# Pipelining three layer boundaries by groups of four slots, with the last channels of the first convolution in two small blocks

## Chip, cores, metric

One core of one Trainium2 chip. The metric is the device time of one execution of the program, in microseconds; the times below are medians of several executions. Before the change it was 617.7 us (three runs, 616.61 to 618.29). A "span" is the time from the first to the last instruction in a profiled execution; it is about 1.8 us shorter than the device time of the same execution.

## The reference, cut

```python
x = u                                              # 2048 positions x 512 channels, bf16
x = x + conv(layernorm(x), A, B, C, log_dt, Dskip)  # long convolution per channel: kernel K from A, B, C
x = x + attn(layernorm(x), wqkv, wo)                # 32 heads of 16, 8 keys at distance 0, 2, .. 14
x = x + conv(layernorm(x), ...)                     # the same convolution again
x = x + attn(layernorm(x), wqkv, wo)                # the same attention again
# conv: y = irfft(rfft(pad(x)) * rfft(pad(K)))[:L] + x * Dskip
```

The kernel runs as four stages: tables and the convolution's spectra together with the first convolution (until about 265 us), attention (until about 402), second convolution (until about 470), attention (until the end). Three boundaries lie between them, and each needs a layer norm over all 512 channels of a position. The state `X` is held as 16 "slots" of 128 positions, `X[:, j, :]`.

## The kernel before: the parts the change touches

The layer norm statistics. `gather` takes statistics of a stretch of channels, `finish` aggregates them and makes scale and bias, `norm` applies them:

```python
    def gather(self, X, part, j0, j1): ...      # nc.vector.bn_stats, one per slot
    def finish(self, j0, j1):
        for j in range(j0, j1):
            nc.vector.bn_aggr(self.mv[:, j, :], ...)
        nc.vector.tensor_copy(self.mvb[:, js], self.mv[:, js])
        nc.vector.tensor_scalar(self.veps[:, js], self.mvb[:, js, 1], EPS, None, ALU.add)
        nc.scalar.activation(self.den[:, js], self.veps[:, js], ACT.Sqrt)
        nc.vector.reciprocal(self.rstd[:, js], self.den[:, js])
        nc.vector.scalar_tensor_tensor(self.nb[:, js], self.mvb[:, js, 0], -1.0, self.rstd[:, js], ...)
```

The end of the first convolution. Channels 448 to 511 are the last "half": tables, contraction into the convolution kernel, spill to memory and refetch in another layout, spectrum `Kt`, products with the signal's spectrum, inverse, final matmuls, then the norm over all 16 slots:

```python
        cv.finish(3, xc, Kt, Xr, 0, 2)          # channels 384..447
        ln_b.gather(X, 0, 0, NJ)                # three quarters of the channels, 16 slots
        Kt = k_fft(3, 1, 2)                     # spectrum of the last 64 channels, at once
        cv.finish(3, xc, Kt, Xr, 2, 4)
        ln_b.gather(X, 1, 0, NJ)
        ln_b.finish(0, NJ)
```

The weights of the attention. The value weights are loaded and re-laid by four VectorE copies, which the scheduler places behind the last statistics:

```python
        nc.scalar.dma_start(wvn[:], wsrc[:, :, 1024:1536])
        for ft in range(4):
            nc.vector.tensor_copy(wv[:, :, ft*128:(ft+1)*128]..., wvn[:, :, ft*128:(ft+1)*128]...)
```

The second convolution, with the norm in front of it and the statistics behind it:

```python
        for j in range(0, NJ, 4): ln.gather(X, 0, j, j + 4)
        ln.finish(0, NJ)
        for j in range(NJ): ln.norm(U[:, j, :], X[:, j, :], j)
        for k in range(16 + 14):
            ...                                  # final, inverse, product, s2, turn, s1, staggered
            if k == 13 + 11: ln_b.gather(X, 0, 0, NJ)
        ln_b.gather(X, 1, 0, NJ)
        ln_b.finish(0, NJ)
```

In the second convolution `U` is the normalised signal, `ps_s` and `Z` the first stage of its transform, `pt` and `zt` its transpose, `xp` and `xc` the second stage, `pa`, `pb` and `Y` the product with the kernel's spectrum `Kt`, `vp` and `VT` the inverse, and `ps_y` the last stage. `psA` is memory of the same kind that several of these steps share. In the attention, 16 normalised slots are transposed (tile `pt_x`), projected to queries and keys (`ps_qk`, evacuated by ScalarE into `qT` and `kT`), multiplied (`prod`), and summed into logits (`Lp`); then come the value projection (`ps_v`), softmax, `po` and the output projection (`ps_o`, evacuated into `X`).

## Time and profile before

| | before |
|---|---|
| time, median of 3 | 617.7 us |
| profiled span | 613.9 us |
| tables end (last `Y2tab` product) | 230.7 |
| first attention: first transpose `pt_x` | 271.7 |
| first output evacuation | 378.6 |
| second convolution: first / last `xp` | 414.2 / 460.7 |
| second attention: first transpose `pt_x` | 478.7 |

The times in the lower rows are microseconds from the start of the span. The page of the kernel before opens with busy time, share of the span and instruction counts by engine:

```profile
span 613.9 us, 13332 instructions
PE 447.4 (73%) x5785; PEld 288.1 (47%) x5785; DVE 508.0 (83%) x921; ACT 337.5 (55%) x452; POOL 12.7 (2%) x49
```

The shares are averages over stages with different limits. The timeline of VectorE (DVE) around the first boundary follows. The columns are start, busy time, engine, line, operation, output<-inputs, shapes, count, and in brackets the idle time in front of it with what ended it.

```profile
230.63 7.45 DVE L140 BATCH_NORM_STATS2 ln_st_b<-X 128x6 f32<-128x384 bf16 x16
...
253.99 2.19 DVE L114 COPY wv<-wvn 128x512 bf16<-128x512 bf16 x4 [13.10 <-DMA wvn<-in_B_wqkv_dram]
256.10 0.68 DVE L254 TENSOR_TENSOR pa<-xc,Kt 128x1024 bf16<-128x1024 bf16 x1
...
265.66 3.19 DVE L140 BATCH_NORM_STATS2 ln_st_b<-X 128x6 f32<-128x128 bf16 x16 [7.08 <-ACT X L270]
268.77 1.28 DVE L145 BATCH_NORM_AGGREGATE ln_mv_b<-ln_st_b 128x2 f32<-128x12 f32 x16
...
271.25 1.70 DVE L153 TENSOR_SCALAR xn<-X,ln_rstd_b,ln_nb_b 128x512 bf16<-128x512 bf16 x5
```

For 13.10 us VectorE stands before the weight copies, whose load has not landed. The last spectrum was complete at 253.73, but the first product `pa` needs only the first of its two casts, which ended at 252.82. So `pa`, which started at 256.10, was held up for 3.3 us: about 1.2 by the load and 2.1 by the copies themselves. After that everything is serial: products, inverse, final matmuls, 16 statistics, 16 aggregates, the small steps, the first norm. TensorE (PE) in the same place:

```profile
256.84 0.40 PE L239 MATMUL psA<-sb_IC,pa 128*128 128x256 bf16 x1 [4.20 <-DVE pa L254]
...
258.06 0.42 PE L239 MATMUL psA<-sb_IC,pa 128*128 128x256 bf16 x1
258.27 0.42 PE L240 MATMUL psA<-sb_IC,pb 128*128 128x256 bf16 x1
```

The matmuls of this kind start 0.21 us apart after the idle time; before it, at full clock, the same matmuls came 0.11 apart. The granted clock was 0.50 from about 255 to 261.8. TensorE's idle time in front of these matmuls was 4.20 us (252.64 to 256.84), and the clock was halved about 2.3 us into it (see the last section).

The boundary to the second convolution, VectorE and then TensorE: 16 norms in a row, and TensorE waits 3.31 us for the first.

```profile
404.70 5.26 DVE L153 TENSOR_SCALAR U<-X,ln_rstd_a,ln_nb_a 128x512 bf16<-128x512 bf16 x16
```

```profile
405.17 1.34 PE L591 MATMUL ps_s_6063<-U,sb_F_128 128*128 128x128 bf16 x8 [3.31 <-DVE U L153]
```

The boundary from the second convolution to the attention, VectorE and then TensorE: 27 statistics and 16 aggregates stand ahead of the first norm, and TensorE idles 8.60 us.

```profile
467.60 8.24 DVE L140 BATCH_NORM_STATS2 ln_st_b<-X 128x6 f32<-128x384 bf16 x27
475.75 1.28 DVE L145 BATCH_NORM_AGGREGATE ln_mv_b<-ln_st_b 128x2 f32<-128x12 f32 x16
...
478.24 1.71 DVE L153 TENSOR_SCALAR xn<-X,ln_rstd_b,ln_nb_b 128x512 bf16<-128x512 bf16 x5
```

```profile
478.71 4.00 PE L693 MATMUL pt_x<-sb_ident,xn 128*128 128x128 bf16 x32 [8.60 <-DVE xn L153]
```

### The profile page before, as it was taken

The numbers are of one execution on the slowest core, as the hardware profiler recorded it, in microseconds if no ns is written. First come the engines' busy times: TensorE is split into PE (matmuls) and PEld (weight loads), VectorE is DVE, ScalarE is ACT, GpSimd is POOL, SyncE is SP. The second block draws the span as 40 slices with busy tenths as digits, with TensorE's granted clock in tenths as the row PEclk, the third lists the DMA queues.
The fourth block names the chain that finished last, engine by engine and source line by source line (L and its number), as shares of the span: only waits on it lengthen the run. The fifth ranks groups of instructions, "written<-read, shape, count | busy, mean of one in ns | idle before, by whom it ended". The sixth has DMA issues, their size and how long they took to land.

```text
span 613.9 us, 13332 instructions
## 1 busy us (share of the span) xinstructions
PE 447.4 (73%) x5785; PEld 288.1 (47%) x5785; DVE 508.0 (83%) x921; ACT 337.5 (55%) x452; POOL 12.7 (2%) x49
## 2 busy tenths in 40 slices
PE   1101867767777777559988679969995799957996
PEld 0101544554564465344333566646773533326763
DVE  5999799999999996265977899768999678879950
ACT  4999357556554654437575223467874456732144
POOL 0000000000000000300000000000000000000000
PEclk9999999898897898879999699979999799977999
DMA  9101001311221042500002100060000000040011
GB/s 292 61 1 34 19 19 37 103 38 36 88 53 36 21 121 72 171 1 1 1 1 82 39 1 1 1 275 1 1 2 1 2 1 0 1 120 1 1 70 68
DMA packets 23048, 28.77 MB, mean 47 GB/s; under 512 B 13009, under 2 KB 18514, under 8 KB 21838
## 3 DMA queue, kind: packets, MB, share of 16 engines
q1 hardware_dynamic: 20590, 26.75, 13.1%
q10 hardware_dynamic: 2400, 1.18, 0.7%
q8 instruction: 45, 0.74, 0.5%
q14 instruction: 13, 0.11, 0.1%
HBM read 15.89 MB, written 8.39 MB: 40 GB/s over the span
## 4 chain that ended last, share of the span: by engine, by line
DVE 49%; PE 34%; issue 8%; ACT 5%; DMA 3%; POOL 0%; SPq 0%; POOLq 0%; DVEq 0%; ACTq 0%
PE ps_qk L711 9%; DVE Ytab L443 5%; PE ps_v L721 5%; DVE ta L412 4%; PE ps_o L835 4%; DVE tb L413 4%; DVE Y2tab L445 4%; PE po L826 2%; DVE Xtab L414 2%; DVE ln_st_b L140 2%; PE Lp L753 2%; DVE Ytab L414 2%; DVE pa L620 2%; DVE pb L621 1%; DVE VT L643 1%
## 5 line engine op out<-in xcount | busy, mean ns | idle before, releaser
L711 PE MATMUL ps_qk<-xnT,wqk 128*128 128x512 bf16 x256 | 63.1, 382 | 0.9 <-ACT kT_4648 L713 0.3
L829 ACT CAST oT<-po 128x1024 bf16<-128x1024 f32 x16 | 15.4, 1015 | 58.7 <-PE po L826 58.7
L187 PE MATMUL psA<-X,sb_F_128 128*128 128x128 bf16 x128 | 15.1, 236 | 36.5 <-ACT X L498 32.6
L187 PEld LDWEIGHTS <-sb_F_128 128*128 128x128 bf16 x288 | 17.6, 99 | 46.8 <-issue 44.1
L835 PE MATMUL ps_o<-wo_t,oT 128*128 128x512 bf16 x128 | 34.6, 380 | 3.4 <-ACT oT L829 2.6
L711 PEld LDWEIGHTS <-wqk 128*128 128x128 bf16 x256 | 22.9, 98 | 29.5 <-issue 8.2
L174 ACT CAST Z<-psA 128x1024 bf16<-128x1024 f32 (+1 forms) x36 | 31.1, 930 | 8.9 <-PE psA L187 8.7
L462 PE MATMUL psk<-Y2tab,Xtab 128*32 128x48 bf16 x1024 | 22.8, 201 | 16.5 <-issue 15.2
L459 PE MATMUL psk<-Ytab,Xtab 128*32 128x64 bf16 x1024 | 24.1, 205 | 12.5 <-DVE Xtab L414 5.5
L753 PE MATMUL Lp<-prod,sb_bones 128*32 128x512 bf16 x256 | 24.7, 392 | 10.3 <-DVE prod L748 7.5
L174 ACT CAST VT<-psA 128x512 bf16<-128x512 f32 x32 | 17.2, 589 | 23.6 <-PE psA L242 23.6
L443 DVE TENSOR_TENSOR Ytab<-Ytab,MA 128x2048 bf16<-128x2048 bf16 x24 | 29.3, 1220 | 0.2
L462 PEld LDWEIGHTS <-Xtab 128*32 128x32 bf16 x1024 | 20.2, 100 | 19.5 <-issue 18.1
L445 DVE TENSOR_TENSOR Y2tab<-Ytab,MB 128x2048 bf16<-128x2048 bf16 x24 | 29.2, 1218 | 0.0
L721 PE MATMUL ps_v<-wv,xnT 128*128 128x512 bf16 x128 | 28.3, 379 | 0.0
L459 PEld LDWEIGHTS <-Xtab 128*32 128x32 bf16 x1024 | 20.7, 103 | 15.0 <-issue 13.6
L140 DVE BATCH_NORM_STATS2 ln_st_b<-X 128x6 f32<-128x384 bf16 (+1 forms) x64 | 21.4, 413 | 7.1 <-ACT X L270 7.1
L838 ACT CAST X<-ps_o 128x512 bf16<-128x512 f32 x32 | 18.3, 586 | 16.0 <-PE ps_o L837 16.0
L202 PE MATMUL pt<-sb_ident,Z 128*128 128x128 bf16 x256 | 21.7, 239 | 7.2 <-ACT Z L174 7.2
L140 DVE BATCH_NORM_STATS2 ln_st_a<-X 128x6 f32<-128x512 bf16 x32 | 21.1, 687 | 7.1 <-ACT X L838 5.3
L465 ACT CAST KTq<-psk 128x1024 bf16<-128x1024 f32 x8 | 8.1, 1013 | 32.1 <-issue 16.6
L693 PE MATMUL pt_x<-sb_ident,xn 128*128 128x128 bf16 x128 | 13.5, 266 | 15.0 <-DVE xn L153 14.8
(462 smaller groups left out, 1311.1 us busy)
## 6 DMA issues: line engine op xcount, KB each, us to landing
Kt<-kt_scratch SPq DMA_DIRECT2D x4, 1024.0 KB, 6.7
Vp<-V SPq DMA_DIRECT2D x2, 1568.0 KB, 9.2
kt_scratch<-Kt SPq DMA_DIRECT2D x3, 1024.0 KB, 4.5
X<-in_A_u_dram SPq DMA_DIRECT2D x4, 512.0 KB, 5.5
Xr<-in_A_u_dram SPq DMA_DIRECT2D x4, 512.0 KB, 4.5
k_scratch<-KTq SPq DMA_DIRECT2D x8, 256.0 KB, 2.1
KT<-k_scratch SPq DMA_DIRECT2D x8, 256.0 KB, 3.6
out_dram<-X SPq DMA_DIRECT2D x4, 512.0 KB, 2.6
```

Source lines behind the costliest of these rows:

```text
L140: self.nc.vector.bn_stats(self.st[:, j, part, :], X[:, j, a:b])
L174: self.nc.scalar.copy(dst, src)
L187: nc.tensor.matmul(o, F1[:, j, r, :], rhs_j(j), start=True, stop=not dk)
L412: nc.vector.tensor_tensor(v(ta), src, self.mult(self.MA, lev, hc, mm), ALU.mult)
L443: nc.vector.tensor_tensor(Y[:, :, :, q * EYB:(q + 1) * EYB, :].rearrange("n c h e t -> n (c h) e t"), src, self.mult(self.MA, lev, hc, EYB ...
L445: nc.vector.tensor_tensor(Y2[:, :, :, (q - 1) * EYB:q * EYB, :].rearrange("n c h e t -> n (c h) e t"), src, self.mult(self.MB, lev, hc, EY ...
L459: nc.tensor.matmul(psk[32 * g:32 * g + 32, ds, :], xs, Y[:, m // 2, h, :, t], start=(m == 0), stop=False, skip_group_check=True)
L462: nc.tensor.matmul(psk[32 * g:32 * g + 32, ds, EYB:], xs, Y2[:, 1 - m // 2, h, :, t], start=False, stop=(m == 3), skip_group_check=True)
L711: nc.tensor.matmul(ps[:], wqk[:, ct, f0:f0 + 128], xnT[:, ct, s0:s0 + 512], start=(ct == 0), stop=(ct == 3))
L721: nc.tensor.matmul(ps[:].rearrange("p a b -> p (a b)"), xnT[:, ct, j * 128:(j + 1) * 128], wv[:, ct, :], start=(ct == 0), stop=(ct == 3))
L753: nc.tensor.matmul(Lp[r0:r0 + 32, w // 4, :], bones[:, w % 4, :], pr[:, f2, hb * 512:(hb + 1) * 512], start=(w % 4 == 0), stop=(w % 4 == 3 ...
L835: nc.tensor.matmul(ps[:], oT[:, ft, j * 128:(j + 1) * 128], wo_t[:, ft, :], start=(ft == 0), stop=False)
```

## The change

The intent is to turn each boundary from "all 16 slots, then the next layer" into four groups of four slots: statistics, aggregate, scale and norm of a group follow as soon as its four slots are final, and the next layer starts on it. In addition the last 64 channels of the first convolution are cut into two blocks of 32 which are contracted, spilled, fetched and transformed separately, with half as many inverse matmuls per block (VectorE combines the two products first). The value weights' copies move to ScalarE, into the place in the program where the value projection starts. A block `with at(tc, mark)` gives instructions an earlier priority for the scheduler, which is how a group's norms are placed in the layer before. The core of the diff:

```diff
@@ load_b_weights
-        nc.scalar.dma_start(wvn[:], wsrc[:, :, 1024:1536])
-        for ft in range(4):
-            nc.vector.tensor_copy(wv[...], wvn[...])
+    nc.sync.dma_start(wvn[:], wsrc[:, :, 1024:1536])
@@ proj_v (in the attention)
+            for ft in range(4 if wvn is not None else 0):
+                nc.scalar.copy(wv[...], wvn[...])
@@ LnStats.finish
-        nc.vector.tensor_copy(self.mvb[:, js], self.mv[:, js])
-        nc.vector.tensor_scalar(self.veps[:, js], self.mvb[:, js, 1], EPS, None, ALU.add)
-        nc.scalar.activation(self.den[:, js], self.veps[:, js], ACT.Sqrt)
+        nc.scalar.activation(self.den[:, js], self.mv[:, js, 1], ACT.Sqrt, bias=self.eps[:, 0:1])
@@ end of the first convolution
-        Kt = k_fft(3, 1, 2)
-        cv.finish(3, xc, Kt, Xr, 2, 4)
-        ln_b.gather(X, 1, 0, NJ)
-        ln_b.finish(0, NJ)
+        T.y_products(Y, Y2, 7, 0, HD // 2)
+        T.y_products(Y, Y2, 7, HD // 2, HD)
+        ...
+            T.contract(Xt, Y, Y2, 7, 0)
+            T.contract(Xt, Y, Y2, 7, 1)
+        ...
+            for u in range(2):
+                nc.sync.dma_start(KT[:, u]..., kscr[7][:, :, u * 128:u * 128 + 128]...)
+                cv.spectrum32(KT[:, u], ..., Kt[:, 2 + u], ...)
+                cv.block(2 + u, xc, Kt, VT)
+        def after(j0, j1):
+            ln_b.gather(X, 2, j0, j1)
+            ln_b.finish(j0, j1)
+            marks.append(room(tc, 40))
+        cv.final(3, 64, 128, Xr, VT, 4, after)
@@ second convolution: norms by groups in front, statistics by groups behind
+        for q in range(4):
+            with at(tc, marks[q]):
+                for j in range(q * 4, q * 4 + 4):
+                    ln.norm(U[:, j, :], X[:, j, :], j)
...
-            if k == 13 + 11:
-                ln_b.gather(X, 0, 0, NJ)
-        ln_b.gather(X, 1, 0, NJ)
-        ln_b.finish(0, NJ)
+            q = k - 13 - 8
+            if 0 <= q < 4:
+                ln_b.gather(X, 0, q * 4, q * 4 + 4)
+            elif 4 <= q:
+                ln_b.gather(X, 1, (q - 4) * 4, q * 4 - 12)
+                ln_b.finish((q - 4) * 4, q * 4 - 12)
+                marks.append(room(tc, 40))
@@ attention: norm and transposes of group q at marks[q]; projections by 512 positions
-            for sh2 in range(2):
-                ...                              # keys and queries of 1024 positions at a time
+            for s0 in range(0, S, 512):
+                ...                              # keys and queries of 512 positions at a time
@@ out (end of the attention)
+                    if ln_next is not None:
+                        ln_next.gather(X, 0, j - 3, j + 1)
+                        ln_next.finish(j - 3, j + 1)
+                        out_marks.append(room(tc, 8))
```

(The rest is the moved `products`, `block` and `final` functions, buffer pools that let the layers overlap, and the second set of statistics tiles.)

## The prediction

> **What bounds it now.** The page gives VectorE 83% busy, TensorE 73%, but the limit changes by stage. In ten-microsecond windows VectorE is 8.8 to 9.9 busy of 10 from 80 to 240 us (tables and first convolution) and about 10 from 420 to 470 (second convolution). TensorE is 9 to 10 of 10 in the first 40 us of each attention layer. Between stages nobody is full, and the chain of waits is serial there:
>
> - First convolution to attention: the last table product ends at 230.6, the first normalised slot for attention starts at 271.25. Between: contraction, spill and refetch (PE starts on it at 245.7), spectrum, and 13.1 us in which VectorE waits for the value-weight load: those copies stand in its queue ahead of the last products, whose spectrum was there by about 253 (waits, timeline). The inverse matmuls then come 0.21 us apart instead of 0.11, granted clock 0.50. [...] PE had idled 4.2 us.
> - Attention to second convolution: TensorE idles 3.3 us, normalising 16 slots takes 5.3, VectorE idles 5 of 410 to 420 while the pipeline fills.
> - Second convolution to attention, 467.7 to 478.2: 27 statistics instructions (8.2 us), 16 aggregates (1.2), six small steps; TensorE idles 8.6 us. From 478.7 it is nearly full.
>
> **What the change does, costed.**
>
> 1. Last 64 channels as two blocks of 32. Each block's contraction, spill, fetch and spectrum start as soon as its tables exist. Cost: products in 24 pieces of 512 elements instead of 6 of 2048 (about 0.36 against 1.14 us), so +1.8 us VectorE; four blocks with a combining subtract and add, +0.82 each. The weight copies (2.2 us and the 13.1 us wait) move to ScalarE. Estimate from the trace's durations: tables end 232.4, second half contracted 234, spilled 237, fetched 241, spectrum 248, products and inverse 252, first group normalisable 255. VectorE's own work until there adds to about 23 us (statistics 10.6, blocks 8.4, evacuations 3.5), a co-limit; with queueing I take 257 to 258. Gain 13.5 us.
> 2. Attention to second convolution: three groups are normalised under the output projection, where VectorE has 5 us of slack (380 to 402). Only the last group's statistics and four norms remain. Gain about 5 us.
> 3. Second convolution to attention: only a quarter of the late statistics (0.8 of 3.2 us) and aggregates (0.3 of 1.2) stand before the first normalisation. The three-quarter statistics stay: VectorE is full before. Gain about 3.5 us. Projection then needs 5.3 us of TensorE per group against 3.6 of VectorE, so it stays TensorE-bound.
> 4. Given back, about 2 us: weight copies on ScalarE under the projections; the new order completes the keys two tiles later, and the products need all keys.
>
> These gaps are all on the chain; the attention interiors (488 to 602) should only shift. Sum: about 20 us, predicted 597.5 us (-3.3%), 8 in 10 between 590 and 606. Faster by over 2% (under 605.3): 0.85; within: 0.13; slower: 0.02.
>
> **What would show each.** 1: first pt_x transposes near 257 instead of 271.7; no VectorE wait on the weight load. 2: TensorE gap under 2 us, VectorE over 7 of 10 there. 3: TensorE gap 8.6 to about 5 us. Attention interiors unchanged within 2 us.
>
> **What would make it wrong.** In-order VectorE: statistics placed ahead of the block products, or a normalisation waiting on memory shared with the previous layer, would cost several us. Two small spectra may leave TensorE idle and at half clock, slowing the projections. If the spill and fetch round trip doubles with its smaller pieces, step 1 loses 4 us.

The sum: 13.5 + 5 + 3.5 - 2 = 20 us. The order of VectorE's queue that the text relies on is in the trace above: the first input of `pa` was ready at 252.82, but `pa` started at 256.10, behind the copies that had waited for their load until 253.99.

## The result, and the profile after

After: 607.82 us, median of 4 (607.30 to 608.56). Before: 617.37, median of 4 (616.61 to 618.29). The ratio is 0.9846, 95% interval 0.9828 to 0.9863. Ratios here are the mean time of one kernel's fast runs over that of the other's of the same rounds, so they are not quite the ratio of the medians. The prediction, 597.5 with a range of 590 to 606, was too fast: the change brought about 9.5 us, not 20. All outputs are right.

In legs (start times of the marker instructions in the two profiles, subtracted):

| leg | before us | after us | gain us | predicted gain us |
|---|---|---|---|---|
| start to tables' end | 230.72 | 233.85 | -3.1 | -1.7 |
| tables' end to first `pt_x` | 41.00 | 30.96 | +10.0 | about +15 |
| (sum of both: first boundary) | 271.72 | 264.81 | +6.9 | +13.5 |
| first `pt_x` to first output | 106.85 | 108.32 | -1.5 | part of -2 |
| first output to first `xp` (second boundary) | 35.58 | 32.81 | +2.8 | +5 |
| first `xp` to last `xp` | 46.56 | 46.56 | 0 | 0 |
| last `xp` to second `pt_x` (third boundary) | 18.00 | 15.33 | +2.7 | +3.5 |
| second `pt_x` to first `Lp` | 20.68 | 23.06 | -2.4 | part of -2 |
| first `Lp` to end | 114.46 | 115.10 | -0.6 | part of -2 |

The legs add to 7.9 us of span. The timed difference is larger because the profiled execution of the kernel before took 615.64 us, 1.7 below its median. The page after opens:

```profile
span 606.0 us, 13365 instructions
PE 445.1 (73%) x5743; PEld 289.0 (48%) x5786; DVE 514.4 (85%) x976; ACT 338.9 (56%) x465; POOL 12.7 (2%) x50
```

VectorE gained about 6 us of work. The first boundary, VectorE:

```profile
250.70 0.69 DVE L337 CAST Kt<-xpu 128x512 bf16<-128x512 f32 x1
...
256.10 1.24 DVE L150 BATCH_NORM_STATS2 ln_st_b<-X 128x6 f32<-128x64 bf16 x9 [2.52 <-ACT X L308]
...
264.41 1.31 DVE L161 TENSOR_SCALAR xn<-X,ln_rstd_b,ln_nb_b 128x512 bf16<-128x512 bf16 x4
```

The wait of 13.10 us is gone. VectorE now waits 2.52 us for ScalarE (ACT), and ScalarE's timeline says why:

```profile
252.44 3.15 ACT L838 COPY wv<-wvn 128x512 bf16<-128x512 bf16 x3
255.49 1.06 ACT L308 CAST X<-psA 128x512 bf16<-128x512 f32 x2
256.45 1.13 ACT L838 COPY wv<-wvn 128x512 bf16<-128x512 bf16 x1
257.46 1.08 ACT L275 CAST VT<-psA 128x512 bf16<-128x512 f32 x2
```

The weight copies sit in ScalarE's queue between two steps of the chain: three of them ahead of the casts that free `psA`, one ahead of the next block's `VT`. The trace shows the wait: the casts of `X` start at 255.49, as the third copy ends, although the last of their matmuls had started at 253.85 and took 0.27 us. TensorE in the same place:

```profile
256.12 0.27 PE L290 MATMUL psA<-sb_IC,y 128*128 128x256 bf16 x1 [2.00 <-ACT X L308]
...
264.81 1.37 PE L809 MATMUL pt_x<-sb_ident,xn 128*128 128x128 bf16 x16 [0.96 <-DVE xn L161]
```

The second boundary, VectorE (answering to the 16 norms at 404.70) and ScalarE:

```profile
399.96 0.18 DVE L157 RECIPROCAL ln_rstd_a<-ln_den_a 128x4 f32<-128x4 bf16 x1 [0.87 <-ACT ln_den_a L156]
...
400.37 1.38 DVE L161 TENSOR_SCALAR U<-X,ln_rstd_a,ln_nb_a 128x512 bf16<-128x512 bf16 x4
```

```profile
397.80 1.94 ACT L699 CAST Z<-ps_s 128x1024 bf16<-128x1024 f32 x2
399.61 0.32 ACT L156 ACTIVATE ln_den_a<-ln_mv_a,eps 128x4 bf16<-128x4 f32 x1
```

Only four norms are left at the end, but the last group's square root stands behind two casts of groups that are already in the convolution.

The third boundary, VectorE and then TensorE (answering to the 27 statistics at 467.60 and the idle 8.60 us):

```profile
454.01 1.93 DVE L150 BATCH_NORM_STATS2 ln_st_b<-X 128x6 f32<-128x384 bf16 x4
...
458.12 0.41 DVE L728 TENSOR_TENSOR Y<-pa,pb 128x512 bf16<-128x512 bf16 x1
...
462.04 4.08 DVE L150 BATCH_NORM_STATS2 ln_st_b<-X 128x6 f32<-128x384 bf16 x11
...
467.42 1.33 DVE L161 TENSOR_SCALAR xn<-X,ln_rstd_b,ln_nb_b 128x512 bf16<-128x512 bf16 x4
...
471.10 1.37 DVE L161 TENSOR_SCALAR xn<-X,ln_rstd_b,ln_nb_b 128x512 bf16<-128x512 bf16 x4
...
479.49 1.39 DVE L161 TENSOR_SCALAR xn<-X,ln_rstd_b,ln_nb_b 128x512 bf16<-128x512 bf16 x4
```

```profile
458.59 0.28 PE L740 MATMUL vp<-sb_IC,Y 128*128 128x256 bf16 x1 [2.97 <-DVE Y L728]
...
467.83 1.44 PE L809 MATMUL pt_x<-sb_ident,xn 128*128 128x128 bf16 x16 [2.93 <-DVE xn L161]
```

The idle time before the transposes fell from 8.60 to 2.93 us as intended. But TensorE now also waits 2.97 us at 458.59, because four statistics at 454.01 and one more stand ahead of the last combine `Y`, and the groups' norms come 3.7 to 4.3 us apart. The last of the convolution's final matmuls ended 5.2 us earlier than before (464.90 against 470.12), while the first `xp` had started 8.2 us earlier (405.94 against 414.15): 3 us of the lead were lost inside the convolution's tail.

So the open questions were: why the first boundary gave 6.9 instead of 13.5; why the second gave 2.8 instead of 5; and why the third gave 2.7 and lost it again.

### The profile page after: what moved, and what is told of

It reads as the page before. It is cut to its first block, busy times and chain, and to the rows that moved or that the text cites. A ratio compares the mean times of both kernels' runs of the same rounds, so it can differ in the third digit from the quotient of the medians.

```text
span 606.0 us, 13365 instructions
## 1 busy us (share of the span) xinstructions
PE 445.1 (73%) x5743; PEld 289.0 (48%) x5786; DVE 514.4 (85%) x976; ACT 338.9 (56%) x465; POOL 12.7 (2%) x50
## 4 chain that ended last, share of the span: by engine, by line
DVE 52%; PE 28%; ACT 9%; issue 8%; DMA 2%; POOL 0%; SPq 0%; POOLq 0%; ACTq 0%; DVEq 0%
PE ps_qk L829 7%; DVE prod L931 6%; DVE ta L479 4%; DVE Y2tab L518 4%; DVE tb L480 4%; DVE Ytab L516 4%; PE ps_o L955 4%; PE ps_v L843 3%; DVE Xtab L481 3%; DVE ln_st_b L150 3%; PE Lp L875 2%; DVE Ytab L481 2%; PE po L946 2%; DVE ln_st_a L150 2%; DVE pa L726 2%
## 5 line engine op out<-in xcount | busy, mean ns | idle before, releaser
L946 PE MATMUL po<-sb_ident,prod 128*128 128x128 bf16 x1024 | 72.7, 232 | 11.4 <-DVE prod L931 7.9
L946 PEld LDWEIGHTS <-prod 128*128 128x128 bf16 x1024 | 65.2, 105 | 20.6 <-DVE prod L931 17.2
L862 DVE TENSOR_TENSOR prod<-qT,kT 128x2048 bf16<-128x2048 bf16 (+3 forms) x48 | 43.2, 953 | 14.0 <-ACT qT L831 7.2
L931 DVE TENSOR_TENSOR prod<-V,L 128x2048 bf16<-128x2048 bf16 (+3 forms) x48 | 43.6, 947 | 6.4 <-PE po L946 6.4
L195 PE MATMUL psA<-X,sb_F 128*128 128x128 bf16 x128 | 14.9, 236 | 36.2 <-ACT X L578 32.3
L870 DVE TENSOR_TENSOR prod<-qT,kT 128x2048 bf16<-128x2048 bf16 (+3 forms) x40 | 34.9, 902 | 6.9 <-ACT kT L831 4.3
L195 PEld LDWEIGHTS <-sb_F 128*128 128x128 bf16 x256 | 16.6, 100 | 45.6 <-issue 42.8
L535 PE MATMUL psk<-Ytab,Xtab 128*32 128x64 bf16 x1024 | 26.1, 214 | 15.6 <-DVE Xtab L481 5.8
L955 PE MATMUL ps_o<-wo_t,oT 128*128 128x512 bf16 x121 | 33.5, 380 | 4.7 <-ACT oT L949 3.9
L931 DVE TENSOR_TENSOR prod<-Vp,L 128x2048 bf16<-128x2048 bf16 (+3 forms) x40 | 34.9, 896 | 0.0
L535 PEld LDWEIGHTS <-Xtab 128*32 128x32 bf16 x1024 | 22.7, 113 | 17.9 <-issue 15.2
L516 DVE TENSOR_TENSOR Ytab<-Ytab,MA 128x2048 bf16<-128x2048 bf16 (+1 forms) x33 | 30.6, 929 | 0.2
L518 DVE TENSOR_TENSOR Y2tab<-Ytab,MB 128x2048 bf16<-128x2048 bf16 (+1 forms) x33 | 30.6, 927 | 0.0
L843 PE MATMUL ps_v<-wv,xnT 128*128 128x512 bf16 x126 | 28.2, 379 | 1.8 <-ACT V L845 1.7
L150 DVE BATCH_NORM_STATS2 ln_st_b<-X 128x6 f32<-128x384 bf16 (+2 forms) x80 | 23.5, 357 | 3.8 <-ACT X L308 3.8
```

Of the source, the lines that this page charges most:

```text
L150: self.nc.vector.bn_stats(self.st[:, j, part, :], X[:, j, a:b])
L516: nc.vector.tensor_tensor(v(Y[:, :, :, q * EYB:(q + 1) * EYB, :]), src, vm(self.mult(self.MA, lev, hc, EYB)), ALU.mult)
L518: nc.vector.tensor_tensor(v(Y2[:, :, :, (q - 1) * EYB:q * EYB, :]), src, vm(self.mult(self.MB, lev, hc, EYB)), ALU.mult)
L535: nc.tensor.matmul(psk[32 * g:32 * g + 32, ds, :], xs, Y[:, m // 2, h, :, t], start=(m == 0), stop=False, skip_group_check=True)
L843: nc.tensor.matmul(ps[:].rearrange("p a b -> p (a b)"), xnT[:, ct, j * 128:(j + 1) * 128], wv[:, ct, :], start=(ct == 0), stop=(ct == 3))
L862: nc.vector.tensor_tensor(pr[:, :, (ja - j0) * 128:(ja - j0) * 128 + n], qT[fp][:, :, ja * 128: ja * 128 + n], kT[fp][:, :, (ja - sh) * 12 ...
```

## The experiments

Sixteen runs were made in four calls on different chips, on which the kernel before took 617.4, 615.9, 615.2 and 616.7 us; so ratios are compared, and medians only inside one call. The quoted expectations use letters for theories. For the first boundary: W says that only the move of the weights matters, S says that the split into blocks of 32 brings a part of its own, and Q says that the weight copies' place in a busy engine's queue eats part of the gain. For the third boundary and the attention: N says that its grouping is worth nothing as it stands, O says that the new order of the projections delays the keys, and D says that VectorE limits the cadence of the groups.

### The change again

> Control: the changed kernel as it is, timed beside the others of this call. All theories: 607 to 609 us, ratio to the kernel before about 0.985; first attention transposes near 265 us, last convolution-2 to attention transposes near 468.

Measured: 607.92 us against 617.41, ratio 0.9857 (0.9834 to 0.9881), span 607.0. It repeats. The profile shows tables ending 1.1 us later than in the first profile of the same kernel, and all later markers shifted by about the same amount; one of two profiles of the kernel before was 2.3 us later in the same way. The table stage moves by one to two microseconds between executions and between variants; differences of that size in one profile mean nothing unless they sit in the leg in question.

### Only the weights, on the kernel before

```diff
-    with tc.tile_pool(name="wtmp", bufs=1) as wtmp:
-        nc.scalar.dma_start(wvn[:], ...)
-        for ft in range(4): nc.vector.tensor_copy(wv[...], wvn[...])
+    wvn = const.tile([128, 4, 512], BF, name="wvn")
+    nc.sync.dma_start(wvn[:], ...)
@@ proj_v
+            for ft in range(4 if wvn is not None else 0): nc.scalar.copy(wv[...], wvn[...])
```

> The kernel before with one part of the change alone: the value weights land in a tile of their own and the four re-ordering copies stand on ScalarE in the value projection instead of on VectorE. Theory W (leg 1 owes its gain to the lifted weight wait): VectorE no longer idles 13 us ahead of the last products, the first attention transposes come 5 to 7 us earlier than 271.7 (265 to 267), total 5 to 6 us shorter (0.990 to 0.992). Rival S (the gain comes from the two blocks of 32): first transposes no more than 3 us earlier, total at most 2.5 us shorter (above 0.996).

Measured: 612.71 us, ratio 0.9935 (0.9912 to 0.9957): 4.7 us by the medians, half of the whole gain. The first transposes came 3.3 us earlier, between what W and S said, so this run alone decides for neither; the next one does. The last spectrum to the first transposes shrank from 18.0 to 13.6 us, which is where the copies had stood. VectorE in this run:

```profile
253.95 0.69 DVE L250 TENSOR_TENSOR pa<-xc,Kt 128x1024 bf16<-128x1024 bf16 x1 [11.73 <-ACT Kt L170]
```

VectorE idles almost as long as before, now for the spectrum, so the 13.10 us as such had cost little. What was gained is the 3.3 us for which `pa` was held up, and about 1.2 us behind it, by estimate the clock's: TensorE's idle time in front of the inverse matmuls fell from 4.20 to 0.96 us, the granted clock stayed at 1.00 from 239.3 to 266.6, and the stretch from the start of `pa` to the first cast of `X` took 7.7 us (253.95 to 261.68) instead of 9.0 (256.10 to 265.05). (The edit also gives the value weights a tile of their own and moves their load, and some of the output weights', to SyncE's queue; load and copies were not separated.)

### The change without the two blocks of 32

```diff
-        T.y_products(Y, Y2, 7, 0, HD // 2)
-        T.y_products(Y, Y2, 7, HD // 2, HD)
+        T.y_products(Y, Y2, 7)
@@
-            T.contract(Xt, Y, Y2, 7, 0)
-            T.contract(Xt, Y, Y2, 7, 1)
+            T.contract(Xt, Y, Y2, 7)
@@ one spill, one fetch, one spectrum of 64 channels, then block(2), block(3)
-                cv.spectrum32(KT[:, u], ...)
+            Z = cv.s1(..., 64, ...); cv.s2(Z, 2, [Kt[:, 2], Kt[:, 3]], "kt")
```

> The changed kernel without the two blocks of 32: tables of the last 64 channels in one piece, one contraction, one spill, one spectrum; all else stays, the grouped layer boundaries too. Theory W: within 1.5 us of the changed kernel either way (606 to 609.5), because the split only trades a later end of the tables against an earlier fetch. Rival S: 3 us or more slower than the changed kernel (over 610.5), first transposes after 267.5.

Measured: 614.12 us, ratio 0.9954 (0.9933 to 0.9975), span 612.1. Without the blocks the change loses about two thirds of its gain; the blocks are worth about 6 us of time here (614.12 against 607.92 on the same chip). The last spectrum was complete 25.7 us after the tables instead of 17.6. So both parts carry the first boundary; theory W, that the weights are all, is refuted by the two runs together.

### The weight copies on GpSimd

```diff
-                nc.scalar.copy(wv[...], wvn[...])
+                nc.gpsimd.tensor_copy(wv[...], wvn[...])
```

> The changed kernel with the four weight copies on GpSimd instead of ScalarE. Theory Q (in the changed kernel these copies, 4.2 us at 252.4 to 257.6, stand in ScalarE's in-order queue ahead of the casts that free PSUM for the last blocks): first transposes 3 to 4.5 us earlier (260.5 to 262), total 3 to 4 us shorter than the changed kernel (604 to 605). Rival V (VectorE's statistics and small steps and the halved clock hold that stretch): at most 1 us shorter.

Measured: 606.52 us (604.12 to 610.52), ratio 0.9845 (0.981 to 0.988): no clear difference from the change. The six executions fall into two groups, three at 604.1 to 604.8 us, as theory Q said, and three at 608.3 to 610.5, with granted clocks of 0.94 and 0.92; why is not known, and the profile is of a slow one (609.98). In it the queue of ScalarE is free of the copies, but VectorE's own combines slow down while GpSimd (POOL) copies. VectorE and then GpSimd:

```profile
254.19 1.33 DVE L284 TENSOR_TENSOR y<-pa,pb 128x512 bf16<-128x512 bf16 x1
...
259.22 0.40 DVE L284 TENSOR_TENSOR y<-pa,pb 128x512 bf16<-128x512 bf16 x1
```

```profile
252.61 5.11 POOL L838 COPY wv<-wvn 128x512 bf16<-128x512 bf16 x4 [1.99 <-DMA wvn<-in_B_wqkv_dram]
```

The same combine takes 1.33 us under the copies and 0.40 after them. It lasts there about as long as one GpSimd copy (5.11 / 4 = 1.28 us); what makes it slower was not shown. The run therefore decides nothing about theory Q: it removed one delay and added another.

### The third boundary in one group

```diff
-                ln_b.finish((q - 4) * 4, q * 4 - 12)
-                marks.append(room(tc, 40))
+        ln_b.finish(0, NJ)
+        marks = [room(tc, 40) for _ in range(4)]
```

> The changed kernel with only the boundary from the second convolution to the second attention layer undone: all statistics, then one finish, then the norms. Theory N (this boundary's grouping buys an earlier first norm and gives it back in a projection that VectorE feeds too slowly): total within 1 us of the changed kernel (607 to 609), first transposes about 3 us later, first logits matmul within 1 us. Rival G (grouping gains 2.5 to 3.5 us as predicted): 610 to 611.5 us.

Measured: 607.97 us against 615.86, ratio 0.988 (0.9866 to 0.9895), span 605.8, against 606.0 and 607.0 of the change. By the ratios (0.9846 and 0.9857 for the change, on other chips) it is 0.2 to 0.3% slower. In the profile the tables ended 0.9 us earlier; counted from the last `xp`, the rest took 154.2 us against 153.5, so 0.7 us are lost. So the grouping at this boundary was worth 0.7 to 2 us, and theory N holds as far as the profiles show. In the run the first transposes came 18.5 us after the last `xp`, 3.2 more than with the groups, and the projection of the first half of the heads (to the 16th cast of `qT` and `kT`) took 21.31 us from there against 23.75. In that stretch TensorE idled 0.44 us against 2.42 (0.39 before the change). TensorE has about 21 us of work to do there at the speed it gets; starting on it earlier in crumbs only moved idle time behind the start.

### The second boundary in one group

```diff
-                        ln_next.finish(j - 3, j + 1)
-                        out_marks.append(room(tc, 8))
+                        if j == NJ - 1:
+                            ln_next.finish(0, NJ)
+                            out_marks.extend(room(tc, 8) for _ in range(4))
```

> The changed kernel with only the boundary from the first attention layer to the second convolution undone: one finish after all 16 slots, then 16 norms. From the traces the grouping is worth 2.7 us from the first output cast to the first second-stage matmul: 610 to 611 us. If the predicted 5 us were right: 612.5 or more. If it is worth nothing: under 608.8.

Measured: 611.35 us, ratio 0.9932 (0.9917 to 0.9947), span 609.0. The first `xp` came at 408.98 instead of 405.94 after the same first output (373.07 and 373.13), and the end at 609.0 instead of 606.0. So in the profiles the grouping at the second boundary is worth 3.0 us, and all of it arrives at the end. The ratios, against the change's 0.9846 and 0.9857 from other chips, say 4.6 to 5.3; no run of the change stood in this call, so 3 to 5 us is what can be said.

### Each group's projection right behind its transposes

```diff
         for q in range(4):
             with at(tc, marks[q]):
                 start(q)
+                proj_qk(0, (q,))
...
-        proj_qk(0)
         qk_products(0)
```

(The marks also got more room, 80 instead of 40.)

> The changed kernel with the first q and k projections of a group issued directly behind that group's transposes in both attention layers, so that ready projection matmuls do not queue behind transposes that wait for VectorE. Theory O [...]: from first transposes to first logits matmul 1.5 to 2.5 us shorter in each attention layer, total 3 to 5 us shorter (603 to 605). Rival D (VectorE is the pace-maker: statistics, norms and transposed copies of about 4 us a group): within 1 us of the changed kernel.

Measured: 612.21 us, ratio 0.9934 (0.9915 to 0.9952): slower than the change. The first `Lp` comes sooner after the transposes in the second attention (19.7 us against 23.1), but the first value projection comes later after it (26.3 against 22.0). The early `Lp` is one group alone, and in the first attention the 16th cast is at 290.56 instead of 286.54: with projections between the transposes TensorE waits for each group's ScalarE copy (0.81 us before the last) and starts slowly, the first 16 matmuls taking 6.57 us where the later groups' 16 take 3.61. The hope in theory O, that a finer order would give the loss back, is refuted.

### Every second norm of the attention on ScalarE

```diff
+                if j % 2 == 0:
                     ln_b.norm(xn[:, j, :], X[:, j, :], j)
+                else:
+                    nc.scalar.activation(xn[:, j, :], X[:, j, :], ACT.Identity,
+                                         bias=ln_b.nb[:, j:j + 1], scale=ln_b.rstd[:, j:j + 1])
```

> The changed kernel with every second normalisation of the attention layers on ScalarE (8 of 16, each about 0.34 us off VectorE). Theory D: a group costs VectorE 0.7 us less, so the projections are fed 2 to 2.7 us sooner at the end of each boundary, total 2 to 5 us shorter (603 to 606). Theory O: no more than 1 us shorter, or longer, since ScalarE also makes the projections' casts.

Measured: 612.61 us, ratio 0.9944 (0.993 to 0.9959). Transposes to first `Lp` became 23.7 us in both attentions (21.0 and 23.1 in the change). ScalarE takes 0.76 us for a norm (1.52 for two in its timeline), VectorE 0.33 (1.31 for four), and ScalarE is the engine that must also copy the transposes and cast the projections. The gain that theory D expected did not come. But the run does not refute that VectorE limits the groups: it relieved one engine by slower work on another that is on the same chain.

### The weight copies on ScalarE, but later

```diff
+                late = small.tile([128, 1], F32, name="late", tag="late")
+                nc.vector.tensor_scalar(late[:], ln_b.nb[:, NJ - 1:NJ], 0.0, None, ALU.mult)
             for ft in range(4 if wvn is not None else 0):
-                nc.scalar.copy(wv[...], wvn[...])
+                nc.scalar.activation(wv[...], wvn[...], ACT.Identity, bias=late[:, 0:1])
```

The bias is zero times a value of the last group's norm, so the copies can't run before the boundary is over.

> The changed kernel with the four weight copies still on ScalarE, but made to depend on the last group's normalisation factors (a bias that is always zero), so they cannot stand ahead of the first convolution's casts and nothing on GpSimd disturbs VectorE. The earlier trial on GpSimd was confounded: while GpSimd copied (252.6 to 257.7), VectorE's 128x512 combine took 1.33 us instead of 0.42. Theory Q (ScalarE's queue): from the end of the tables to the first transposes 27 to 28.5 us instead of 31.0, total 2 to 4 us shorter than the changed kernel (ratio to before 0.979 to 0.982). Rival V (chain of small steps on VectorE and a half-speed TensorE): 30 us or more, total at most 1 us shorter (0.984 or above).

Measured: 608.54 us against 615.24, ratio 0.9892 (0.9878 to 0.9907). The first transposes came 28.2 us after the tables instead of 31.0: the queue did cost 2.8 us there. But the first `Lp` stayed where it was (286.02 against 285.84), and the total did not improve: by the ratios (0.9892 against 0.9846 and 0.9857) it is 2 to 3 us longer, in the profile equal. The four copies now stand among the projections' casts. ScalarE and then TensorE:

```profile
274.95 1.24 ACT L841 ACTIVATE wv<-wvn,late 128x512 bf16<-128x512 bf16 x1
276.07 0.60 ACT L831 CAST kT<-ps_qk 128x512 bf16<-128x512 f32 x1
276.54 1.24 ACT L841 ACTIVATE wv<-wvn,late 128x512 bf16<-128x512 bf16 x1
```

```profile
276.72 1.02 PE L829 MATMUL ps_qk<-xnT,wqk 128*128 128x512 bf16 x4 [0.56 <-ACT kT L831]
```

Between two copies there is room for one cast; with two buffers for `ps_qk`, TensorE waits 0.56 to 0.71 us four times. The cost was real and was only moved.

### The statistics of the second convolution group by group

```diff
-            if 0 <= q < 4:
-                ln_b.gather(X, 0, q * 4, q * 4 + 4)
-            elif 4 <= q:
+            if 4 <= q:
+                ln_b.gather(X, 0, (q - 4) * 4, q * 4 - 12)
                 ln_b.gather(X, 1, (q - 4) * 4, q * 4 - 12)
                 ln_b.finish((q - 4) * 4, q * 4 - 12)
```

The three-quarter statistics of a group now come just before the rest of that group, instead of all 16 ahead of the first.

> The changed kernel with the three-quarter statistics of the second convolution issued group by group, directly ahead of the same group's last-quarter statistics, instead of all of them ahead of the first group. Theory D (at this boundary VectorE's order decides when TensorE is fed): first transposes 2 to 4 us earlier than 467.8, the last ps_y matmul about 2 us earlier (in the changed kernel nine statistics stand ahead of the last combines), first logits matmul 2 to 4 us earlier than 490.9, total 2 to 3.5 us shorter (ratio 0.980 to 0.982). Rival: VectorE's total work up to the last group is the same, so the projection ends when it did and the total stays within 1 us (0.984 to 0.988).

Measured: 602.30 us (601.46 to 602.90), ratio 0.9786 (0.9773 to 0.9799), span 601.1. This is faster than the change by 0.6 to 0.7% in the ratios and 4.9 us in the spans, with one small move. VectorE:

```profile
457.63 1.93 DVE L150 BATCH_NORM_STATS2 ln_st_b<-X 128x6 f32<-128x384 bf16 x4
...
460.08 2.27 DVE L150 BATCH_NORM_STATS2 ln_st_b<-X 128x6 f32<-128x384 bf16 x7
...
463.64 1.33 DVE L161 TENSOR_SCALAR xn<-X,ln_rstd_b,ln_nb_b 128x512 bf16<-128x512 bf16 x4
```

The first `xp` came 0.7 us later than in the change, the first group's norm 3.8 us earlier. TensorE's waits around it, by stretches of three microseconds: start and end, length, busy time of TensorE with the number of matmuls, weight loads, VectorE, ScalarE, GpSimd, then the granted clock. First the change, then this run:

```profile
467.00:470.00 3.00, 1.44 (x16) 1.01 (x17) 3.00 (x16) 0.64 (x1) 0.00 (x0) 0.83 0.00 0
470.00:473.00 3.00, 2.35 (x6) 0.90 (x7) 2.31 (x13) 1.45 (x4) 0.00 (x0) 0.50 0.01 3
473.00:476.00 3.00, 3.00 (x21) 2.18 (x20) 1.97 (x8) 1.12 (x2) 0.00 (x0) 0.53 0.02 5
```

```profile
467.00:470.00 3.00, 3.00 (x13) 1.28 (x12) 2.40 (x8) 0.70 (x2) 0.00 (x0) 0.60 0.01 3
470.00:473.00 3.00, 2.92 (x25) 1.58 (x23) 2.45 (x11) 2.48 (x5) 0.00 (x0) 1.00 0.02 5
473.00:476.00 3.00, 3.00 (x27) 1.84 (x26) 3.00 (x11) 1.47 (x4) 0.00 (x0) 1.00 0.00 0
```

In the same nine microseconds the change put 43 matmuls and transposes (of different sizes) through TensorE, this run 65. The 16th cast came at 486.72 instead of 491.58. This is what the third boundary had lost: the statistics that grouping should have taken off the chain were still all on it, some in front of the convolution's last combines.

The profiles of all runs bear this out. From the last `xp` to the end of the last `ps_y` took 9.4 us in the kernel before and in all five profiles with the new order, and 12.3 to 12.5 in every run that kept the change's order. Part of the gain came by way of the clock: between the last `xp` and the 16th cast TensorE stood at half clock for 10.2 us in the change and for 3.4 in this run. Two pairs of profiles with the same code at this boundary show what that is worth: 37.65 us with 6.8 us at half clock (late copies on VectorE) against 39.08 with 10.2 (the change), and 32.27 with none against 33.62 with 3.4 (the two profiles of the next combination). That is 1.4 us for each 3.4, so an estimated 2.8 of the 5.5 us by which this stretch shrank.

### Both: ordering and late copies on ScalarE, and the kernel before once more

> Both edits of the two runs above together. If both theories hold the gains add: 4 to 7 us shorter than the changed kernel (ratio 0.974 to 0.979). If only one holds, as that one alone.

Measured: 605.27 us, ratio 0.9822 (0.9798 to 0.9847), slower than the ordering alone, although its profile was the fastest so far: span 598.3, from the one execution that took 600.11 us. The five others took 604.73 to 605.64. Not settled by this run; see its repeat below.

> The kernel before once more, for a second profile: the first profiled execution took 615.6 us, its timed runs 617.4, so the stages of the first profile may be up to 2 us too short. Expected 615 to 618 us, the stages within 1 us of the first profile except one or two.

Measured: one look at the kernel before, unchanged: 617.94 us, span 616.2 against 613.9 in the first profile. The 2.3 us lie before the first transposes (274.05 against 271.72); from there to the end both take 342.1 us. So the leg table's first rows carry an uncertainty of this size; the others agree in these two profiles.

### The weight copies on VectorE, late

The shortfall of the first boundary was still open: was it recoverable, or would it always reappear in the projections? VectorE is idle between the last norms and the first logit products.

```diff
             for ft in range(4 if wvn is not None else 0):
-                nc.scalar.copy(wv[...], wvn[...])
+                nc.vector.tensor_scalar(wv[...], wvn[...], late[:, 0:1], None, ALU.add)
```

> The changed kernel with the four value-weight copies on VectorE, made to wait for the last statistics of the boundary (a bias that is zero times the last group's result), so that no engine that is on the chain of the first boundary has them in front of it, and the projections' casts on ScalarE don't either; VectorE has gaps between about 275 and 285 us. Theory Q (the copies' place in a queue costs about 2.7 us of the first boundary, and the run with late copies on ScalarE only moved that cost into the projections): tables' end to first transposes 27 to 29 us, first transposes to first Lp at most 22, ratio to the kernel before 0.978 to 0.984. Rival (the first boundary's end doesn't set the first Lp; the projections are limited by something else, so that an earlier start gains nothing): transposes to first Lp 23 to 24 and ratio 0.986 to 0.990, as with the late copies on ScalarE (0.989).

Measured: 604.84 us against 616.74, ratio 0.9819 (0.98 to 0.9838). Tables' end to transposes 29.5 us, half a microsecond outside what theory Q said, but transposes to first `Lp` 19.9, inside it, and the ratio inside. The rival, an attention that gains nothing from an earlier start, is refuted. That the first leg is 29.5 and not 28.2, as with late copies on ScalarE, is not the copies' doing: the spectra took 18.5 us instead of 17.5, and the combination that was profiled twice shows both values for one kernel. VectorE:

```profile
273.28 2.46 DVE L841 TENSOR_SCALAR wv<-wvn,late 128x512 bf16<-128x512 bf16 x4
277.29 3.03 DVE L866 TENSOR_TENSOR prod<-qT,kT 128x2048 bf16<-128x2048 bf16 x4 [1.55 <-ACT qT L831]
```

The four copies take 2.46 us in a gap that still has 1.55 us left after them: on this engine, at this time, they are free. The first `Lp` is at 283.5 us, against 285.8 and 286.9 in the two profiles of the change.

### Ordering and late VectorE copies

```diff
@@ both edits: the statistics group by group, and the copies as in the run above
```

> The late VectorE copies together with the statistics of the second convolution issued group by group. If the two are independent: the gain of the ordering alone over the changed kernel (about 0.9 per cent) plus what the late VectorE copies give by themselves (theory Q 0.3 to 0.6 per cent), ratio 0.971 to 0.977. If the rival holds, as the ordering alone, 0.977 to 0.981. If late copies have a cost of their own that only shows in timed runs (as with late copies on ScalarE and the ordering: profile 598, timed 605), above 0.981.

Measured: 600.22 us (599.50 to 601.39), ratio 0.9743 (0.9721 to 0.9764), span 599.1. This beats both kernels and is the best. The two gains add.

> The ordering alone, repeated on the chip of the two runs above, so that best3 is compared on the same chip. It measured 0.9786; 0.977 to 0.981 expected.

Measured on the same chip: 602.62 us (601.67 to 603.91), ratio 0.9781 (0.9758 to 0.9804). The ordering repeats, and the late copies on VectorE are worth 2.4 us on top of it, with ranges of the runs that do not meet.

> Repeat of the ordering with late copies on ScalarE, whose runs were 600.1 once and 604.7 to 605.6 five times. If the two times are two speeds of the same program, both show again (one near 0.975, others near 0.983). If the 600.1 was a stray, all are near 0.983. If 605 belonged to that chip, all are near 0.975 here.

Measured: 603.24 us (601.02 to 604.18), ratio 0.9785 (0.9759 to 0.981). Neither of two tidy speeds: four runs spread over 3 us. What holds is that late copies on ScalarE add nothing to the ordering; why the first runs lay at 605 stays open.

## Why the prediction was wrong, point by point

**What bounds the kernel: right.** The boundaries were serial, and what was taken off their chains arrived at the end (second boundary: 3.0 us earlier start, 3.0 us earlier end). The interior of the second convolution took 46.56 us in both. The first attention from transposes to first output changed by 1.5 us and the second from its first `Lp` on by 0.6, within the 2 us said; the second with its projections took 3.0 us longer, and that is step 3 below.

**Step 1, the first boundary: 13.5 predicted, 6.9 measured. This term failed most.** The prediction was a sum of three pieces, and each was too small. The sums are shown by the profiles:

| kernel | tables' end | tables to last spectrum | spectrum to first `pt_x` | first `pt_x` |
|---|---|---|---|---|
| before | 230.7 | 23.0 | 18.0 | 271.7 |
| weights only | 232.0 | 22.8 | 13.6 | 268.4 |
| change without blocks | 232.3 | 25.7 | 11.0 | 269.0 |
| prediction | 232.4 | 15.6 | about 9.5 | 257.5 |
| after | 233.9 | 17.6 | 13.4 | 264.8 |
| copies late on ScalarE | 234.0 | 17.5 | 10.6 | 262.1 |
| copies late on VectorE | 234.0 | 18.5 | 11.0 | 263.6 |

Of the 7.3 us by which `pt_x` missed 257.5, 1.5 come from later tables, 2.0 from the spectra, 3.9 from the last piece. Of those 3.9, 2.4 to 2.8 are the weight copies in ScalarE's queue, shown by the two runs that moved them. The prediction named them, but as a cost "under the projections"; the scheduler put them in the middle of the chain. The product pieces cost close to what was estimated (24 of them in 8.1 us, against 6.9 for the six large ones). The rest of the tables' delay is within the wobble of that stage. The remaining 1.1 to 1.5 us of the last piece were not separated; half clock is not their cause, since with late copies on ScalarE none of this piece ran at half clock and it still took 10.6 us. The spectra are another matter, and the prediction's warning that two small spectra may leave TensorE at half clock came true: in the change they ran at 0.50 from 243.7 to 247.1. In the six profiles in which this stretch of half clock was 6.8 us long instead of 3.4 (and the contraction ran at full clock), tables to last spectrum took 18.5 us instead of about 17.5. So the clock moves this piece by a microsecond; how much of the 2.0 us is its doing was not separated.

The signs that the prediction asked for came half: the wait on the weight load was gone, and `pt_x` came at 264.8, not near 257.

**Step 2, the second boundary: 5 predicted, 2.8 in the leg, 3.0 in the profile of the run that undid it (up to 5 by its ratio).** The mechanism was right: the norms on the chain fell from 5.26 to 1.38 us, 3.9 less. The mis-sized term is what stays: the last group's square root waits behind two casts (1.94 us), and TensorE still idles 2.44 us at 400.84, waiting for the cast behind it (under 2 was predicted), and then runs at half clock (0.50 from 401 to 404). VectorE in 410 to 420 went from 5.02 to 10.00 busy, as predicted.

**Step 3, the third boundary: 3.5 predicted, 2.7 at the transposes, nothing at the end.** The step of the prediction that failed is "The three-quarter statistics stay: VectorE is full before." They were not a constant. Ahead of the first group they cost the convolution's tail 3 us and delayed the first group by 1.5 more. The next sentence, that the projection "stays TensorE-bound" behind the groups, failed with it: TensorE idled 2.42 us in that stretch instead of 0.39. The ordering run shows the term's size. From the last `xp` to the 16th cast of queries and keys, the whole boundary with its projections, the kernel before took 39.4 us (460.71 to 500.08), the change 39.1 (452.50 to 491.58), the ordering run 33.5 (453.19 to 486.72). Of these 5.5 us, about 3.0 lie in the convolution's tail, 1.5 between it and the first transposes, 1.1 behind them. The spans differ by 4.9 us, the ratios by 0.6 to 0.7%, so about 4 to 5 us. The predicted idle time, about 5 us, was 2.93: smaller than said, with no gain, because it came back in pieces. The prediction's own warning, "statistics placed ahead of the block products ... would cost several us", described this, for the wrong boundary and without a number in the sum.

**Step 4, given back: 2 predicted, 1.5 + 2.4 + 0.6 = 4.5 in the legs.** Of the 2.4, which belong to step 3, the ordering run took back 1.1 (transposes to 16th cast 22.7 us against 23.75, before 21.4). The rest, the 1.5 and the 0.6 were not taken apart. The key order, which the prediction blamed, could not be improved by the one other order tried.

**The whole.** Predicted 20, measured 9.5. The two causes that the runs isolated, 4 to 5 us of statistics order and 2.4 us of copies, make up 6 to 7 of the missing 10.5; with both mended the kernel took 600.22 us, 16.5 less than the kernel before on that chip, and inside the predicted range. The rest is spread over the second boundary (up to 2.2) and the first one's spectra (2.0), each predicted too fast.

## What to carry to other kernels

Pipelining a boundary moves only the work that comes per group; work that is still issued for all groups at once, like the statistics here, stays on the chain and may even land in the tail of the layer before (12.3 to 12.5 us here instead of 9.4), so issue each group's whole chain together. A copy that "moves to another engine" takes a place in that engine's queue, here in the middle of the chain, where it cost 2.4 to 2.8 us: look for an engine that is idle at a stated time, and pin the copy there with a data dependence, then check the stage behind it as well as the one in front. And an earlier start of a TensorE-bound stage is worth only as much as TensorE can then be kept fed: compare its idle time inside the stage (2.42 us in the change, 0.39 before) and the clock that it was granted (0.50 for 10.2 us in the change, for 3.4 in the ordering run), not the time of its first instruction.

## What the traces of this case show of the hardware

- In the kernel before, the granted clock fell to 0.50 about 2.3 us into an idle time of 4.20 us. In the ordering run the longest idle time before such a stretch was 1.47 us, and the clock was 0.50 from 466.5 to 469: in the 3.5 us before, TensorE had been busy about 1.4 us. What sets the moment was not shown.
- In the run with the copies on GpSimd, 128x512 combines with two inputs took 1.33 us while a GpSimd copy ran (1.28 us each) and 0.40 after the copies.
- All three boundaries turn on the batch-norm statistics and aggregate instructions. Here one statistics instruction took 0.47 us for 384 elements (7.45 / 16), 0.20 for 128 (3.19 / 16), and one aggregate 0.08 (1.28 / 16).
- One kernel's stages move between executions: the tables ended 1.1 us apart in two profiles of the change, and the first transposes started 2.3 us apart in two of the kernel before, which is as much as several of the effects looked for.
